# Reordering the first loads and moving the visit of the single row block in a tuned TensorE-bound kernel

## The chip, the cores and the metric

One core of one Trainium2 chip. The metric is the device time of one execution in microseconds (us), lower is better.

## The reference

Two stages on `x` of shape (8, 4224, 192). The first is a causal convolution over 7 tokens with softmaxed taps per head; the second mixes tokens with two 4224 x 4224 matrices.

```python
def _attn_ref(x, weight):                       # x (8, 4224, 192), weight (8, 7)
    w = softmax(weight)                         # (cut: written out in the reference)
    x_pad = np.concatenate([zeros(B, 6, D), x], axis=1)
    x_unf = x_pad[:, idx, :].reshape(B, S, K, H, group)
    return np.einsum('hk,bskhg->bshg', w, x_unf).reshape(B, S, D)

def _moe_ref(x, w_theta, w_tok_r, w_tok_i, w_ch):
    theta = x @ w_theta
    zr, zi = x * np.cos(theta), x * np.sin(theta)
    y = np.einsum('ts,bsd->btd', w_tok_r, zr) + np.einsum('ts,bsd->btd', w_tok_i, zi)
    u = x + y
    return u + np.maximum(u @ w_ch, 0.0)
```

## The kernel before

The source tokens are cut into 33 chunks of 128, the output tokens into 33 row blocks of 128. The row blocks are visited in units: 16 pairs and one single block (the last, block 32). A **step** is one visit of one unit. There are 58 steps; the units come round in turn, and each chunk is active for 17 consecutive steps, so that it meets every row block once. At most 11 chunks are active at a time. A step runs, for each active chunk, 14 `y` matmuls for a pair or 8 for the single block. Partial sums that have to wait for a later visit go to DRAM (`part`) and come back.

```python
    base = [0, 0, 1, 1, 2, 3, 3, 4, 4, 5, 5]
    start = [base[k % NW] + (NU + 1) * (k // NW) for k in range(NK)]   # first step of chunk k
    NSTEP = start[-1] + NU                                             # 58; NU = 17, NW = 11
    shift = (NU - 1 - (NSTEP - 1)) % NU        # the single block is visited in the last step
    ...
    def active(t):
        return [k for k in range(NK) if start[k] <= t < start[k] + NU]
    def unit(t):
        return (t + shift) % NU                # unit 16 is the single block
```

A chunk is prepared one step ahead: its `x` rows are loaded (`xw`, line 197, issued by GpSimd), convolved (`pc`, line 210, TensorE), multiplied with the angle weights (`v`, line 141) and turned into `z` (ScalarE and VectorE). Each step also loads two matrices of token weights (`st`, line 323, issued by GpSimd), which VectorE transposes (`wt`, line 336) and adds (line 348).

The residual `x` is added to a row block's sum at some time. For the units of the last round (`late`) this is done ahead of time, in DRAM, by accumulating DMAs that GpSimd issues. The step in which they are issued follows from the step number of the unit's last visit:

```python
                    far = known <= start[2 * NW - 1]
                    self.ahead.append((i, 2 * NU - NW + 2 * (t % NU) if far else start[-1],
                                       (t // NU - 1 - far) % 2))
    ...
        def add_ahead(self, i, which):
            tb = self.tbs[i]
            for cols in (slice(0, HN), slice(HN, N)):
                pool(nc.gpsimd.dma_start(                              # line 395
                    out=part[which][tb, :, cols], in_=xs[tb * P : (tb + 1) * P, cols],
                    accum_op=ALU.add,
                ))
```

While a step's matmuls are emitted, events are mixed in at given sevenths of the step:

```python
    def step_events(t):
        ...                                    # weight tasks, row loads, adds: cut
        here = [(r, i, which) for r in steps for i, when, which in r.ahead if when == t]
        for j, (r, i, which) in enumerate(here):
            found.append((1.5 + 1.8 * j, lambda r=r, i=i, which=which: r.add_ahead(i, which)))
        if t + 2 < NSTEP:
            nxt = steps[t + 2]
            for m in (1, 2):
                found.append((1.3 + 3 * (m - 1), lambda m=m: nxt.load_w(m)))
        ...                                    # outputs: cut
        if t >= NU - 2:
            new = [k for k in range(NK) if start[k] == t + 2 and k >= NW]
            for k in new:
                found.append((4.5, lambda k=k: load_chunk(k)))         # x loads
            at = 0.1
            for k in (k for k in range(NK) if start[k] == t + 1 and k >= NW):
                pos = [0, .5, 1.4, 2.2, 2.6, 3.1, 3.15, 3.4, 3.6]      # preparation of chunk k
                ...
                at += 2.3
```

Weight loads, accumulating DMAs and GpSimd's adds are chained to each other in program order (`pool(...)`); the `x` loads are not, and a scheduler places them among the others. The start-up loads `x` of chunks 0 and 1, both weights of step 0, then `x` of chunk 2, both weights of step 1; it then goes through the first 11 chunks one by one.

Of the kernel before, what the change touches and what calls it, by code (L numbers as in the profile page):

```python
# [16 lines left out]
def kernel(  # L17
# [42 lines left out]
    NU = (NT + 1) // 2  # L60
# [4 lines left out]
    assert len(base) == NW  # L65
    start = [base[k % NW] + (NU + 1) * (k // NW) for k in range(NK)]
    NSTEP = start[-1] + NU
    shift = (NU - 1 - (NSTEP - 1)) % NU

    NOSYNC = mybir.DependencyInfo(  # L70
        mybir.DependencyClass.NoSync, mybir.DependencyReason.DATA
# [203 lines left out]
    def load_chunk(k):  # L275
        if k < NK and k not in chunks:
            chunks[k] = Chunk(k, before=chunks[k - 1] if k % NW else None)
# [229 lines left out]
    steps = [Step(t) for t in range(NSTEP)]  # L507
# [72 lines left out]
    def idle(n):  # L580
        for _ in range(n):
            pe(nc.tensor.matmul(
                spare[:, 0, 0:BH], lhsT=noise[:, 0:P], rhs=noise, start=True, stop=True
            ))
# [55 lines left out]
    def more(n):  # L640

        for i in range(n):
            if need[0] is None:
                need[0] = next(flow, NK)
            if need[0] > ready[0]:
                return n - i
            need[0] = next(flow, NK)
        return 0

    steps[0].load_rows()  # L650
    for m in (1, 2):
        steps[0].load_w(m)
    load_chunk(2)
    for m in (1, 2):
        steps[1].load_w(m)
    for i in range(NW + 2):
        ch = chunks.get(i) if i < NW else None
        old = chunks[i - 1] if 0 < i <= NW else None

        def between(n):  # L660
            left = more(n)
            if 0 < i < 3:
                idle(min(left, 2))

        if ch:
            ch.conv(0)
        between(2)
        if old:
            old.theta(0)
        between(1)  # L670
        if ch:
            ch.conv(1)
        if i == 0:
            idle(4)
        ready[0] = i - 2
        between(2)
        if old:
            old.theta(1)
        if i == 1:
            for _, f in steps[0].w_tasks():  # L680
                f()
        if i + 3 < NW:
            load_chunk(i + 3)
        between(1)
        if ch:
            ch.transpose()
        if old:
            old.product(Z11)
        between(2)
        if old:  # L690
            old.product(Z21)
        between(1)
        if old:
            old.sums(0)
        between(1)
        if old:
            old.sums(1)
        between(1)
# [37 lines left out]
```

## Time and profile before

| | before |
|---|---|
| median time | 1449.51 us (1448.77 to 1449.61, 3 runs) |
| profiled span | 1446.4 us |
| TensorE busy | 1416.3 us |
| step 4 begins at | 109.17 us |
| steps 36, 40, 41: length | 26.85, 19.73, 25.67 us |
| end of step 55's y matmuls (S) | 1413.25 us |
| last y matmul ends | 1431.38 us |

A step's begin and end are found by counting the `y` matmuls (line 443) in order of time; its length here runs from the start of its first to the end of its last. The prediction below reads the rest. One more view helps: the timeline of TensorE inside step 40, the only middle step that prepares chunks while it visits the single block (start, duration, engine, line, operation, out<-in, count; in brackets the idle time before, and what ended it):

```profile
1008.71 0.83 PE L141 MATMUL v<-wth,uT 128*128 128x192 f16 x8 [0.30 <-ACT uT L151]
1011.23 0.82 PE L141 MATMUL v<-wth,uT 128*128 128x192 f16 x8 [0.48 <-ACT z L246]
```

A step on the single block has fewer `y` matmuls, so the chain that prepares a chunk (convolve, copy, transpose, copy, multiply) has less other work to hide behind, and TensorE waits for ScalarE between its links (0.30 and 0.48 us in the two rows above).

### The profile page before, as it was taken

How to read it: one execution, taken by the hardware profiler on the slowest of the kernel's cores; microseconds unless marked ns; L12 is line 12 of the kernel's file. 1: busy time of each engine (PE TensorE's matmuls, PEld its weight loads, DVE VectorE, ACT ScalarE, POOL GpSimd, SP SyncE). 2: the span in 40 equal slices, each digit the busy share in tenths (PEclk: the TensorE clock that was granted, in tenths of full speed). 3: DMA queues.
4: the chain of work that ended last, by engine and by line, in shares of the span. 5: the costliest groups of instructions: out<-in, count | busy, mean ns of one | idle time of the engine just before them, and what ended most of it. 6: DMA issues, size and time to landing. Idle time of an engine off the chain costs nothing.

```text
span 1446.4 us, 23748 instructions
## 1 busy us (share of the span) xinstructions
PE 1416.3 (98%) x9809; PEld 887.9 (61%) x9809; DVE 979.2 (68%) x1051; ACT 315.5 (22%) x379; POOL 435.1 (30%) x655
## 2 busy tenths in 40 slices
PE   7899999999999999999999999999999999999997
PEld 5556666666666666666666666666666666666665
DVE  6893555545548777866666657877777667767686
ACT  5861101111134254000000004435210110010133
POOL 7431211111233232432433342233323123213120
PEclk9999999999999999999999999999999999999999
DMA  9986756465699998998899989999999999998893
GB/s 173 227 178 145 146 103 149 90 149 97 137 231 219 214 250 217 228 254 183 213 256 213 242 143 245 228 188 234 279 216 206 209 204 221 204 203 194 166 222 125
DMA packets 272029, 281.99 MB, mean 195 GB/s; under 512 B 106672, under 2 KB 240176, under 8 KB 271920
## 3 DMA queue, kind: packets, MB, share of 16 engines
q0 software_dynamic: 162464, 92.15, 48.4%
q1 hardware_dynamic: 71824, 178.88, 35.1%
q10 hardware_dynamic: 37632, 9.44, 4.1%
q8 instruction: 77, 1.26, 0.3%
q14 instruction: 32, 0.26, 0.1%
HBM read 245.49 MB, written 108.13 MB: 244 GB/s over the span
## 4 chain that ended last, share of the span: by engine, by line
PE 89%; DVE 4%; DMA 3%; POOL 2%; ACT 1%; issue 1%; SPq 0%; DVEq 0%; ACTq 0%; POOLq 0%
PE y L443 82%; PE v L141 5%; PE pc L210 1%; PE tp L165 1%; POOL st L323 1%; DMA xw<-in_x_dram 1%; DVE z L257 1%; DVE wt L336 1%; DVE pv L408 1%; ACT z L246 1%; DVE z L251 0%; DVE pv L476 0%; DVE wt L348 0%; POOL xw L197 0%; DMA xs<-z 0%
## 5 line engine op out<-in xcount | busy, mean ns | idle before, releaser
L443 PE MATMUL y<-z,wt 128*128 128x384 f16 x7656 | 1283.6, 326 | 10.6 <-DVE pv L408 7.5
L443 PEld LDWEIGHTS <-wt 128*128 128x128 f16 x7656 | 740.8, 98 | 488.6 <-issue 10.6
L408 DVE TENSOR_TENSOR pv<-y,pv 128x768 f32<-128x768 f32 x324 | 308.9, 954 | 323.6 <-PE y L443 282.8
L336 DVE STREAM_TRANSPOSE wt<-st 128x1408 f16<-128x1408 f16 (+7 forms) x224 | 327.8, 1465 | 48.5 <-PE y L443 39.0
L323 POOL DMA_DIRECT2D st<-in_moe_w_tok_r_dram x232 | 132.5, 578 | 466.1 <-DVE wt L336 461.0
L323 POOL DMA_DIRECT2D st<-in_moe_w_tok_i_dram x232 | 132.7, 578 | 404.4 <-DVE wt L336 388.9
L348 DVE TENSOR_TENSOR wt<-wt 128x1408 f16<-128x1408 f16 (+7 forms) x216 | 176.7, 818 | 40.8 <-PE y L443 38.4
L151 ACT ACTIVATE z<-pc 128x768 f16<-128x768 f32 x65 | 53.2, 819 | 387.2 <-PE pc L210 386.9
L151 ACT ACTIVATE ub<-pv 128x768 f16<-128x768 f32 x63 | 50.2, 835 | 333.0 <-DVE pv L408 310.4
L406 ACT ACTIVATE pv<-y 128x768 f32<-128x768 f32 x66 | 54.0, 819 | 282.0 <-PE y L443 282.0
L141 PEld LDWEIGHTS <-uT 128*128 128x128 f16 x1056 | 91.0, 98 | 25.8 <-issue 7.9
L386 POOL TENSOR_TENSOR pv<-pv,xr 128x1536 f32<-128x1536 f32 x24 | 74.5, 3105 | 68.6 <-DVE pv L476 22.1
L197 POOL DMA_DIRECT2D xw<-in_x_dram x132 | 76.4, 585 | 31.0 <-DMA xw<-xw 8.7
L476 DVE SCALAR_TENSOR_TENSOR pv<-v,pv 128x768 f32<-128x768 f32 x66 | 62.9, 954 | 27.5 <-PE v L141 27.1
L257 DVE TENSOR_TENSOR z<-z 128x768 f16<-128x768 f16 x132 | 73.4, 556 | 3.6
L151 ACT ACTIVATE uT<-tp 128x1536 f16<-128x1536 f16 (+1 forms) x48 | 58.2, 1215 | 74.4 <-PE tp L165 74.4
L246 ACT ACTIVATE z<-v,half_pi 128x768 f16<-128x768 f32 x66 | 59.8, 907 | 41.2 <-PE v L141 40.8
L251 DVE TENSOR_TENSOR z<-z 128x1536 f16<-128x1536 f16 x66 | 60.0, 947 | 7.5 <-ACT z L246 7.5
L141 PE MATMUL v<-wth,uT 128*128 128x192 f16 x528 | 55.0, 248 | 4.4 <-ACT z L246 3.0
L141 PE MATMUL v<-wch,uT 128*128 128x192 f16 x528 | 54.2, 246 | 2.1 <-DVE pv L476 1.2
L246 ACT ACTIVATE z<-v 128x768 f16<-128x768 f32 x66 | 53.4, 809 | 0.0
L210 PE MATMUL pc<-xw,bands 96*64 96x192 f16 x528 | 35.8, 258 | 2.6 <-ACT bands L625 1.1
(44 smaller groups left out, 142.4 us busy)
## 6 DMA issues: line engine op xcount, KB each, us to landing
part<-pv SPq DMA_DIRECT2D x79, 768.0 KB, 4.3
pv<-part SPq DMA_DIRECT2D x79, 768.0 KB, 6.1
out_dram<-pv SPq DMA_DIRECT2D x66, 384.0 KB, 4.3
st<-in_moe_w_tok_r_dram POOLq DMA_DIRECT2D x136, 176.0 KB, 5.5
st<-in_moe_w_tok_i_dram POOLq DMA_DIRECT2D x136, 176.0 KB, 5.1
xs<-z SPq DMA_DIRECT2D x132, 96.0 KB, 4.5
xw<-in_x_dram POOLq DMA_DIRECT2D x121, 96.0 KB, 6.1
xr<-xs SPq DMA_DIRECT2D x24, 384.0 KB, 3.7
```

The lines of the kernel that those rows point to most:

```text
L141: pe(nc.tensor.matmul(v[:, k, b * D : (b + 1) * D], lhsT=tT[:, 3 * k + b + i, :], rhs=w[:, 2 * b + i, :], start=(i == 0), stop=(i == 1),))
L151: act(nc.scalar.activation(out=out, in_=in_, func=AT.Copy))
L197: nc.gpsimd.dma_start(out=self.xw[lo : lo + n, h, :, :], in_=x[:, t0 : t0 + n, :].rearrange("b s d -> s b d"),)
L246: act(nc.scalar.activation(**args))
L257: dve(nc.vector.tensor_tensor(out=z[:, o, :], in0=z[:, a, :], in1=z[:, b, :], op=ALU.subtract))
L323: pool(nc.gpsimd.dma_start(out=st[a * Q : (a + 1) * Q, 0:nb, :, 0:n] .rearrange("i r bt s -> i (r bt) s"), in_=w[self.tbs[0] * P : (self.t ...
L336: dve(nc.vector.transpose(self.w[name][:, 0 : self.n, :, :], self.st[int(name[1])][:, int(name[0]) - 1, :, 0 : self.n * Q] .rearrange("p b ...
L348: dve(nc.vector.tensor_tensor(out=self.w[name][:, 0 : self.n, :, :], in0=self.w[a][:, 0 : self.n, :, :], in1=self.w[b][:, 0 : self.n, :, : ...
L386: ins = pool(nc.gpsimd.tensor_tensor(out=self.pv[i], in0=self.pv[i], in1=self.xr[i], op=ALU.add))
L408: dve(nc.vector.tensor_tensor(out=o, in0=yv, in1=o, op=ALU.add))
L443: pe(nc.tensor.matmul(y[cn][:, q, 0:BH], lhsT=self.w[wn][:, c, :, :].rearrange("p bt i -> p (bt i)"), rhs=chunks[k].z[:, zn, q * BH : (q + ...
L476: dve(nc.vector.scalar_tensor_tensor(out=ub, in0=channel_mix(self.uT[i][:, 6 * g : 6 * g + 6, :], wch), scalar=0.0, in1=ub, op0=ALU.max, o ...
```

## The change

Its intent is twofold. In the front, `x` of chunk 2 is loaded between the two weight loads of step 0 and `x` of chunk 3 right after them, since the convolution of chunk 3 waits for its `x` (0.88 us in the profile before); five of VectorE's weight tasks of step 0 are put off until after the first product of chunk 0. In the rotation, `shift` grows by one, so that the single block is visited in the last step but one, and a pair comes last: the idea is to have less matmul work behind the last pair's long chain of output work.

```diff
-    shift = (NU - 1 - (NSTEP - 1)) % NU
+    shift = (NU - 1 - (NSTEP - 2)) % NU
...
     steps[0].load_rows()
-    for m in (1, 2):
-        steps[0].load_w(m)
+    steps[0].load_w(1)
     load_chunk(2)
+    steps[0].load_w(2)
+    load_chunk(3)
     for m in (1, 2):
         steps[1].load_w(m)
...
         if i == 1:
-            for _, f in steps[0].w_tasks():
-                f()
+            for at, f in steps[0].w_tasks():
+                if at < 2.2:
+                    f()
...
             old.product(Z11)
         between(2)
+        if i == 1:
+            for at, f in steps[0].w_tasks():
+                if at >= 2.2:
+                    f()
```

## The prediction

The forecast's sum is -0.2 (front) + 2.1 (middle) + 2.1 (end) = +4.0 us, 1453.5 us. Its 0.162 us for one `y` matmul is measured (42 in a row take 6.99 us).

> **What bounds the kernel now.** I read the busy shares and the chain first, then TensorE's waits by stretch, then timelines of the three stretches in which it waits. The page:
>
> ```profile
> PE 1416.3 (98%) x9809; PEld 887.9 (61%) x9809; DVE 979.2 (68%) x1051; ACT 315.5 (22%) x379; POOL 435.1 (30%) x655
> PE   7899999999999999999999999999999999999997
> ...
> PE 89%; DVE 4%; DMA 3%; POOL 2%; ACT 1%; issue 1%; SPq 0%; DVEq 0%; ACTq 0%; POOLq 0%
> ...
> L443 PE MATMUL y<-z,wt 128*128 128x384 f16 x7656 | 1283.6, 326 | 10.6 <-DVE pv L408 7.5
> ```
>
> TensorE is busy 98% and is 89% of the chain; only the first, second and last slices are thinner. A program of the same matmuls can therefore win or lose only where TensorE waits: 1446.4 - 1416.3 = 30 us in all. I counted y matmuls in time order (14 per active chunk in a step on a pair of row blocks, 8 in the step on the single block) to find where each of the 58 steps begins. Steps 4 to 36, from 109 to 922 us, have almost no gap. What is left is the front (0 to 109 us), step 40, and the end from about 1413 us.
>
> The front, TensorE's and VectorE's timelines:
>
> ```profile
> 26.58 0.24 PE L210 MATMUL pc<-xw,bands 96*64 96x192 f16 x1 [0.22 <-ACT z L246]
> 27.70 0.52 PE L210 MATMUL pc<-xw,bands 96*64 96x192 f16 x7 [0.88 <-DMA xw<-in_x_dram]
> 28.15 0.83 PE L141 MATMUL v<-wth,uT 128*128 128x192 f16 x8
> ```
>
> ```profile
> 15.35 0.76 DVE L336 STREAM_TRANSPOSE wt<-st 128x256 f16<-128x256 f16 x2
> 16.15 0.29 DVE L348 TENSOR_TENSOR wt<-wt 128x256 f16<-128x256 f16 x1
> ...
> 19.71 0.96 DVE L149 COPY uT<-tp 128x1536 f16<-128x1536 f16 x1 [1.58 <-PE tp L165]
> ...
> 25.59 0.96 DVE L149 COPY uT<-tp 128x1536 f16<-128x1536 f16 x1 [0.20 <-PE tp L165]
> ...
> 32.85 0.96 DVE L251 TENSOR_TENSOR z<-z 128x1536 f16<-128x1536 f16 x1 [1.57 <-ACT z L246]
> ```
>
> The convolution of chunk 3 waits 0.88 us for x: that is the wait that the first part of the change aims at. VectorE has two holes around it, 1.58 us before 19.71 and 1.57 us before 32.85, and is full between them.
>
> Two single-block steps (23, then 40) and the pair step before 40, in the table of stretches:
>
> ```profile
> 579.44:593.91 14.47, 14.47 (x92) 8.71 (x90) 12.25 (x12) 0.00 (x0) 5.14 (x5) 1.00 1.08 290
> 975.87:1002.72 26.85, 26.85 (x218) 17.30 (x215) 17.58 (x23) 12.33 (x14) 9.17 (x16) 1.00 1.10 227
> 1002.56:1022.29 19.73, 18.64 (x163) 11.77 (x162) 17.60 (x20) 12.22 (x14) 4.57 (x8) 1.00 1.00 309
> ```
>
> The columns are length, then busy us of PE, PEld, DVE, ACT, POOL. Only step 40 leaves TensorE idle (19.73 - 18.64 = 1.09 us).
>
> The end:
>
> ```profile
> 1423.43 0.95 DVE L408 TENSOR_TENSOR pv<-y,pv 128x768 f32<-128x768 f32 x1
> 1424.43 0.48 PE L443 MATMUL y<-z,wt 128*128 128x384 f16 x2 [0.36 <-DVE pv L408]
> 1429.06 2.33 PE L443 MATMUL y<-z,wt 128*128 128x384 f16 x12 [0.22 <-DVE pv L408]
> 1440.19 1.82 DVE L476 SCALAR_TENSOR_TENSOR pv<-v,pv 128x768 f32<-128x768 f32 x2 [0.91 <-PE v L141]
> ```
>
> Here y matmuls wait for VectorE to take earlier sums out of PSUM, and after the last of them a chain of casts, transposes and output sums runs to 1442.0; the last store ends the span at 1446.4.
>
> [...] the eight v matmuls of 28.15 had their operand at 26.55 (25.59 + 0.96) and yet stood behind the convolution that waited. [...] 42 in a row here take 6.99 us with 0.33 for the last, (6.99 - 0.33) / 41 = 0.162 us each. [...] a run of y matmuls waits for the reader of its tile (7.5 us in all, in the page's line). [...]
>
> **The change part by part.** The instructions are the same in number; the built program of after has TensorE's order unchanged until the middle.
>
> *Front.* GpSimd issues x of chunk 2 between the two weight loads of step 0 and x of chunk 3 right after them (from 20.96 to about 14.7 us), so x should be there at 26.58 and the 0.88 us go. But VectorE's five later weight tasks of step 0 (two transposes, three sums) move from the free time at 16.36 to behind the first product of chunk 0. They cost, start to start, 0.47 + 0.53 + 0.48 + 0.29 = about 1.7 us. Before, VectorE had 0.20 us to spare at 25.59; now the copy of chunk 2's transpose starts at 25.59 - 0.20 + 1.7 = 27.1 and ends at 28.0, and the v matmuls that need it start at 28.1, against 28.15. The wait for x turns into a wait for that copy. At 32.85 the hole of 1.57 us swallows the delay. Gain: about 0.2 us, an estimate.
>
> *The single block in the middle.* It is visited at steps 5, 22, 39, 56 in place of 6, 23, 40, 57. From the program's list of starts, the chunks then active are 11, 9, 9, 4 in place of 11, 11, 9, 2: both sum to 33, so the matmuls are equal. But new chunks are prepared during steps 22 and 39 (two each), where before only step 40 had any. What such a step loses I take from step 40: 72 y matmuls are 11.68 us; a pair step with two chunks takes 26.85, of which 126 y are 20.44, so two chunks cost 6.41; 19.73 - 11.68 - 6.41 = 1.64 us lost. Step 41 takes 25.67 where steps 7 to 15 take 25.19: 0.48 more. Together 2.1 us per event. Two events in place of one: +2.1 us.
>
> *The end.* Let S be the end of step 55's y matmuls (1413.25 before). Before, 72 y follow S (56 + 16); after, 60 (32 + 28). So S comes 12 x 0.162 = 1.95 us later. What follows S: before it was 28.75 us to the last vector instruction. After, in the built order: all is as before until VectorE's sum at S + 10.2 to 11.1 (the 1423.43 row), which frees a y tile. From there VectorE has the seven sums of step 57 with one output sum and one cast among them: 8 x 0.92 + 0.5 = 7.9 us, to S + 19.1; before, the last such sum ended at 1432.6 = S + 19.35. After the last y both programs have 30 transposes, 48 v matmuls and six output sums, two tiles alternating. Walking through them with 0.81 for ACT's copies, 0.95 for an output sum and 0.75 for eight v, I come to S + 28.9. So the 12 matmuls less after S buy nothing, since they lay beside vector work. End: 1.95 + 0.15 = +2.1 us.
>
> Sum: -0.2 + 2.1 + 2.1 = +4.0 us; 1449.5 + 4.0 = 1453.5 us.
>
> **The rivals.** (1) *The x wait really goes*: VectorE does the five tasks sooner than I walked, and 0.88 + 0.22 = 1.1 us come through. For: x was on the chain until 27.66. Against: the full VectorE to 28 us, and after it ACT and DVE without holes to 36 and 43 us. It would make 1452.6. (2) *The short step loses nothing at 22 or 39*, since step 40's loss may lie in what came with it (it prepares weights of 11 chunks for step 41: four transposes of 1.64 and four sums of 0.88 are 10.1 us of VectorE; step 39 of the changed kernel prepares 9 chunks). Then 1451.4 to 1452.5. (3) *The end is bound by TensorE*, so that the 12 matmuls count: 1451.4. (4) *A new DMA wait*: step 1's second weights are now held by the deferred transposes until about 23 us, and x of chunk 4 goes out 2.4 us later, landing near 34 by the 31.67 of before; its convolution starts at 36.72. If it slips further, 1 to 3 us are lost: 1455 to 1456.
>
> **Range and chances.** All terms are a few us, against 29 us for 2%. Rivals 1 to 3 together would bring it to about 1450; rival 4 to 1456.5. Range 1450.0 to 1456.5. Faster by over 2%: 0.005, since it is nearly the whole idle time of TensorE; within 2%: 0.985; slower: 0.01.
>
> **What would show it.** Right: no wait for x before chunk 3's convolution near 27, but its v matmuls still at 28.1 with a wait for the DVE copy; step 4 beginning within 1 us of 109.17; steps 22 and 39 each near 19.7 us long with gaps before v matmuls; the last y matmul 2 us later than 1431.4, and seven vector sums back to back before it. Wrong: step 4 beginning 2 us or more earlier (the front was bound by x after all), steps 22 and 39 without gaps, or a tail after S under 31 us (33.2 before).

## The result, and the profile after

The changed kernel took 1457.95 us in the median (1457.18, 1458.73, 1459.21 and 1453.50), the kernel before 1449.14 us in the same rounds (1448.48 to 1449.61, 4 runs). The ratio is 1.0056, 95% interval 1.0033 to 1.0078. Ratios here and below are the mean time of one kernel's runs over that of the other's of the same rounds, so not quite the ratio of the quoted medians. The class "within 2%" came true; the time lies 1.45 us above the upper end of the predicted range. The profiled run has a span of 1455.2 us, 8.8 us longer than before. All outputs are right.

The page of the changed kernel, in the order of the lines that the prediction showed (busy time by engine, shares of the chain that ended last, groups of instructions with their idle time and its main releaser), and below it one line of the view of waits by cause (total us, number of waits, longest):

```profile
PE 1418.4 (97%) x9809; PEld 887.8 (61%) x9809; DVE 976.7 (67%) x1051; ACT 315.1 (22%) x379; POOL 434.3 (30%) x655
...
PE 86%; DVE 6%; ACT 3%; DMA 3%; issue 1%; SPq 0%; POOL 0%; DVEq 0%; ACTq 0%; POOLq 0%
...
L443 PE MATMUL y<-z,wt 128*128 128x384 f16 x7656 | 1285.1, 326 | 12.2 <-DVE pv L408 9.1
L210 PE MATMUL pc<-xw,bands 96*64 96x192 f16 x528 | 35.9, 258 | 5.0 <-DMA xw<-in_x_dram 3.4
```

```profile
PE pc L210 <- DMA xw<-in_x_dram: 3.4, 1, 3.4
```

The counts are the same, but TensorE was busy 2.1 us longer for the same matmuls, and it has one new wait of 3.4 us for `x`. In the kernel before the same cause stands at 0.9 us, once, in the front. **It is now one wait, and not in the front.** There, the two stretches that the prediction described read as follows (TensorE, then VectorE):

```profile
27.84 0.83 PE L141 MATMUL v<-wth,uT 128*128 128x192 f16 x8 [0.98 <-DVE uT L149]
```

```profile
26.87 0.92 DVE L149 COPY uT<-tp 128x1536 f16<-128x1536 f16 x1
```

The convolution no longer waits for `x`; the eight `v` matmuls behind it wait 0.98 us for VectorE's copy instead. Step 4 begins at 108.88 us, 0.29 earlier.

Three steps of the changed kernel in the table of stretches: 22 and 39 (single block, two chunks prepared in each), then 36 (a pair). The columns are the stretch and its length, busy us (and instructions) of PE, PEld, DVE, ACT and POOL, the granted clock, the share of the DMA engines and GB/s:

```profile
552.47:572.20 19.73, 18.64 (x164) 11.78 (x162) 17.60 (x20) 12.21 (x14) 4.56 (x8) 1.00 1.04 321
984.95:1004.67 19.72, 18.64 (x162) 11.77 (x161) 16.18 (x20) 12.21 (x14) 7.49 (x14) 1.00 0.99 241
899.50:931.62 32.12, 28.69 (x217) 17.91 (x215) 22.51 (x28) 12.32 (x14) 9.11 (x16) 0.95 1.04 230
```

Steps 22 and 39 are what step 40 was before, as predicted. Step 36 is not: before, it took 26.85 us with no gap; now 32.12. Its TensorE timeline:

```profile
903.62 0.52 PE L210 MATMUL pc<-xw,bands 96*64 96x192 f16 x7 [3.43 <-DMA xw<-in_x_dram]
904.07 2.61 PE L443 MATMUL y<-z,wt 128*128 128x384 f16 x10
```

The wait itself is 3.43 us, and the ten `y` matmuls right after it take 2.61 us, where ten took 1.80 at this place before. The stretches of the wait and of what follows it say why (the third number from the end is the granted clock, 1.00 being full speed):

```profile
899.50:903.60 4.10, 0.69 (x5) 0.20 (x2) 2.98 (x4) 0.00 (x0) 2.27 (x4) 1.00 1.36 225
903.60:908.00 4.40, 4.38 (x27) 2.18 (x28) 0.00 (x0) 1.31 (x2) 0.00 (x0) 0.65 1.20 347
```

The granted clock was 0.65 over the 4.4 us after the wait; the trace's clock record has it at 0.50 for 3.41 us, from 904.90. So step 36 loses 32.12 - 26.85 = 5.27 us: 3.43 of wait and 1.84 of slower matmuls.

Why `x` came late is read from GpSimd's timeline, first of the kernel before, then of the changed one, at the same place (step 35, where `x` of the chunks that start at step 37 is issued):

```profile
878.08 2.29 POOL L197 DMA_DIRECT2D xw<-in_x_dram  x4
890.38 2.29 POOL L323 DMA_DIRECT2D st<-in_moe_w_tok_i_dram  x4 [10.02 <-DVE wt L336]
```

```profile
881.86 3.46 POOL L395 DMA_DIRECT2D part<-xs  x4
888.61 1.22 POOL L197 DMA_DIRECT2D xw<-in_x_dram  x2 [3.29 <-DMA st<-in_moe_w_tok_r_dram]
894.18 2.28 POOL L323 DMA_DIRECT2D st<-in_moe_w_tok_i_dram  x4 [4.34 <-DVE wt L336]
896.44 0.58 POOL L197 DMA_DIRECT2D xw<-in_x_dram  x1
898.16 0.57 POOL L197 DMA_DIRECT2D xw<-in_x_dram  x1 [1.13 <-DMA part<-xs]
```

Before, all four `x` loads of the first chunk were issued ahead of the second weight load, so its wait of 10.02 us for VectorE cost them nothing; the last of them landed at 888.49, 7.6 us before the convolution began (896.12). After, four accumulating DMAs (line 395) stand first; only two of the four `x` loads come ahead of the weight load, and the other two stand behind its wait for VectorE's transpose (4.34 us). The last is issued at 898.16, when the convolution wants `x` at about 900.2; it lands at 903.57. The accumulating DMAs also hold the loads back directly: they take 3.46 us to issue, the first `x` load then waits 3.29 us for a landing, and so even the two loads in front landed only at 899.26 and 899.47.

Where do the accumulating DMAs come from? From the rotation. Pair [0, 1], which before was visited for the last time in step 41 and had its residual added by GpSimd on an earlier visit, is now the unit of the last step, 57. That makes it `late`, and the rule `2 * NU - NW + 2 * (t % NU)` gives 34 - 11 + 2 x 6 = 35 for it. Before, the rule gave steps 27, 29 and 31, and the other case step 41. Step 35 is one in which chunks are loaded and prepared.

The end, VectorE and TensorE of the changed kernel:

```profile
1432.43 2.81 DVE L408 TENSOR_TENSOR pv<-y,pv 128x768 f32<-128x768 f32 x3
1436.49 4.73 DVE L408 TENSOR_TENSOR pv<-y,pv 128x768 f32<-128x768 f32 x5
```

```profile
1438.55 1.67 PE L443 MATMUL y<-z,wt 128*128 128x384 f16 x8 [0.25 <-DVE pv L408]
```

S, the end of step 55's `y`, is now at 1422.23 us. From 1432.43 (S + 10.2) to 1441.22 (S + 19.0) VectorE is full, and the last `y` matmuls wait for it; from S to the end of the span it is 32.97 us, against 33.15 before.

| | before | after |
|---|---|---|
| step 4 begins | 109.17 | 108.88 |
| step 24 begins | 593.74 | 597.54 (+3.80) |
| step 36 length | 26.85 | 32.12 (+5.27) |
| S | 1413.25 | 1422.23 (+8.98) |
| S to end of span | 33.15 | 32.97 (-0.18) |

### The profile page after: what moved, and what is told of

Same layout as the page of the kernel before. It is cut to its first block, busy times and chain, and to the rows that moved or that the text cites. A ratio compares the mean times of both kernels' runs of the same rounds, so it can differ in the third digit from the quotient of the medians.

```text
span 1455.2 us, 23747 instructions
## 1 busy us (share of the span) xinstructions
PE 1418.4 (97%) x9809; PEld 887.8 (61%) x9809; DVE 976.7 (67%) x1051; ACT 315.1 (22%) x379; POOL 434.3 (30%) x655
## 4 chain that ended last, share of the span: by engine, by line
PE 86%; DVE 6%; ACT 3%; DMA 3%; issue 1%; SPq 0%; POOL 0%; DVEq 0%; ACTq 0%; POOLq 0%
PE y L443 78%; PE v L141 5%; DVE pv L408 1%; ACT z L246 1%; PE pc L210 1%; PE tp L165 1%; DVE z L257 1%; DVE z L251 1%; DVE wt L336 1%; DVE wt L348 1%; DMA xw<-xw 1%; DMA xs<-z 1%; ACT uT L151 1%; ACT z L151 0%; DMA pv<-part 0%
## 5 line engine op out<-in xcount | busy, mean ns | idle before, releaser
L348 DVE TENSOR_TENSOR wt<-wt 128x1408 f16<-128x1408 f16 (+7 forms) x216 | 173.5, 803 | 43.5 <-PE y L443 41.1
L476 DVE SCALAR_TENSOR_TENSOR pv<-v,pv 128x768 f32<-128x768 f32 x66 | 62.9, 954 | 28.1 <-PE v L141 27.8
```

The source lines that it names most:

```text
L348: dve(nc.vector.tensor_tensor(out=self.w[name][:, 0 : self.n, :, :], in0=self.w[a][:, 0 : self.n, :, :], in1=self.w[b][:, 0 : self.n, :, : ...
```

## The experiments

Two theories at the start. **A: an order effect.** The residual additions that the rotation moved to step 35 push part of the `x` loads behind a weight load that waits for VectorE, and everything else of the prediction holds. **B: the rotation itself** costs more than predicted (short steps, tail), or the front part does, and the wait in step 36 is only a slip of a profile. Within A there were two more rivals: that the accumulating DMAs delay `x` in proportion to their traffic, or through waits for their landings (the changed kernel's profile shows one of 1.13 us before the last `x` load), rather than by the order.

**1. The additions of step 35 back to step 33** (changed kernel):

```diff
-  self.ahead.append((i, 2 * NU - NW + 2 * (t % NU) if far else start[-1],
+  self.ahead.append((i, min(2 * NU - NW + 2 * (t % NU), 33) if far else start[-1],
```

> The changed kernel, with the two residual adds of the last pair (four accumulating DMAs) issued in step 33 in place of step 35. Theory A (those four DMAs stand in GpSimd's queue ahead of the x loads for chunk preparation in step 36, and x comes too late): the 3.4 us wait for x in step 36 is gone, step 36 is 26.85 us long again (32.12 in the changed kernel), and the time falls to 1451.5 to 1453 us, 2.5 to 4 us over before. Rival B (the rotation as a whole loads the DMA engines more in steps 35 and 36, the adds are incidental): the wait stays at 2 us or more, time 1455 or over. Steps 22 and 39 stay 19.73 us, and from the end of step 55's y matmuls to the end of the span stays 33 us, under both.

Measured: 1452.72 us (1452.11 to 1454.02), before 1449.02, ratio 1.0030 [1.0015, 1.0045]. Step 36 is 26.85 us long again with no wait for `x`; steps 22 and 39 remain 19.73. The 5.27 us are gone, and the rotation costs what was predicted for it.

**2. The front part alone** (before, with the changed start-up):

```diff
-    shift = (NU - 1 - (NSTEP - 2)) % NU      # against the changed kernel
+    shift = (NU - 1 - (NSTEP - 1)) % NU
```

> The kernel before with the first part of the change alone (x of chunks 2 and 3 earlier, five weight tasks of step 0 later). If the wait for x only turns into a wait for the VectorE copy: step 4 begins 0.1 to 0.4 us earlier than in before (109.17), time 1448.8 to 1449.4, the same within noise. If the rival is right that the front is bound by x: step 4 begins at 108.3 or earlier, time 1448.3 or less.

Measured: 1448.23 us (1448.06 to 1449.25), ratio 1.0000 [0.9985, 1.0014]; step 4 begins at 109.04 us (109.17 before). The begin of step 4 is what the first reading expected; the median lies in the range set for the rival, but with a ratio of 1.0000 the times decide neither. A gain of a few tenths can neither be shown nor excluded. Across all profiles taken, step 4 began anywhere between 106.6 and 111.1 us, whatever the start-up. Whether the clock has a part in that was not shown: the profiles of the kernel before and of the changed one each have one stretch before step 4 in which the granted clock was 0.50, 3.41 us long (from 38.87 and from 37.91).

**3. The rotation alone** (before, with `NSTEP - 2`):

```diff
-    shift = (NU - 1 - (NSTEP - 1)) % NU
+    shift = (NU - 1 - (NSTEP - 2)) % NU
```

> The kernel before with the second part alone (the single block in the last step but one). If the two parts do not touch each other: as the changed kernel plus 0.3 us, 1454 to 1459 us, with the wait for x in step 36, steps 22 and 39 at 19.73 us. If the stall needs the changed front: no wait in step 36, about 1452.5.

Measured: 1456.20 us (1454.72 to 1460.16), ratio 1.0057 [1.0040, 1.0074], the same as the whole change. Its profile, TensorE in step 36:

```profile
905.12 0.52 PE L210 MATMUL pc<-xw,bands 96*64 96x192 f16 x7 [2.75 <-DMA xw<-in_x_dram]
```

The wait is 2.75 us here, and ten `y` matmuls after it took 1.80 us; step 36 is 29.86 us long. So the loss belongs to the rotation, and after this wait the granted clock was 1.00 (over 905.12 to 909.50).

**4. No rotation, but one pair's additions in step 35** (before; they are moved there from step 31):

```diff
-  self.ahead.append((i, 2 * NU - NW + 2 * (t % NU) if far else start[-1],
+  self.ahead.append((i, 2 * NU - NW + 2 * (t % NU) + 4 * (t == 55) if far else start[-1],
```

> The kernel before, with its two residual adds of step 31 (four accumulating DMAs) moved to step 35, nothing else. Theory A: the stall appears here too, step 36 longer than 26.85 us by 2 to 6 us, time 1451.5 to 1455. Rival B: no stall, 1449.1 as before.

Measured: 1455.08 us (1451.34 to 1456.44), before 1449.02, ratio 1.0040 [1.0021, 1.0058].

```profile
900.90 0.85 PE L210 MATMUL pc<-xw,bands 96*64 96x192 f16 x7 [4.43 <-DMA xw<-in_x_dram]
```

The kernel before, with nothing but four DMA issues moved by four steps, has the same wait at the same place, 4.43 us; step 36 is 33.81 us long, 6.96 more than before where 2 to 6 was expected, and the granted clock over the 4.1 us that followed the wait was 0.50. In GpSimd's order two of the four `x` loads stand behind the second weight load, as in the changed kernel. That is the cause without the change, and with experiment 1 the change without the cause.

**5. The additions stay in step 35, but behind the x loads** (changed kernel):

```diff
-  found.append((1.5 + 1.8 * j, lambda r=r, i=i, which=which: r.add_ahead(i, which)))
+  found.append((1.5 + 1.8 * j + 3.5 * (t == 35), lambda r=r, i=i, which=which: r.add_ahead(i, which)))
```

> The changed kernel with the four accumulating DMAs still in step 35, but 3.5 sevenths of the step later, so that the built order has them behind all eight x loads and the second weight load of that stretch. If the place in GpSimd's in-order queue is what counts (with the waits on landings that the built program puts on the loads behind them): no wait for x in step 36, time 1451.5 to 1453.5, and at most 1 us in steps 37 and 38, whose x loads now stand behind them. If it is the added traffic of 1.5 MB in that stretch: a wait for x of 2 us or more remains in steps 36 to 38, time 1455 or over.

Measured: 1453.44 us (1451.75 to 1454.09), before 1449.72, ratio 1.0029 [1.0014, 1.0044]. No wait for `x`; steps 36, 37 and 38 take 26.85, 26.91 and 26.85 us. The same DMAs in the same step are harmless when they are issued later.

**6. Half of the additions in step 35, half in 33** (changed kernel):

```diff
+  self.ahead.append((i, min(2 * NU - NW + 2 * (t % NU), 33 + 2 * i) if far else start[-1],
```

> The changed kernel with the residual adds of one of the two row blocks (two accumulating DMAs) in step 35 and the other's in step 33. In the built order of GpSimd the four x loads then stand ahead of the second weight load, as in before; with all four adds in step 35 two of the x loads had come to stand behind it. If that order is the cause: no wait for x in step 36 (0.3 us at most), time 1452 to 1453.5. If the delay grows with the traffic put ahead: about half the stall, a wait of 1 to 2.5 us, time 1453.5 to 1455.

Measured: 1452.34 us (1451.98 to 1453.50), before 1449.19, ratio 1.0019 [1.0005, 1.0032]; no wait, step 36 is 26.85 us. With two accumulating DMAs the built order has all four `x` loads ahead of the weight load. But the last of them landed at 895.32, 4.6 us before the convolution began (899.92), where the kernel before had 7.6 us to spare. A delay that grows with the DMAs in front is there too, hidden as long as time is left, so this run alone does not separate the order from the traffic.

**7. All additions in step 35 and in front, but the x loads forced ahead of the second weight load** (changed kernel; this separates the place in the order from the traffic of the accumulating DMAs and the waits for landings, which experiment 5 had moved too):

```diff
-  nc.gpsimd.dma_start(                                     # x loads
+  (pool if start[k] == 37 else (lambda ins: ins))(nc.gpsimd.dma_start(
...
-  found.append((4.5, lambda k=k: load_chunk(k)))
+  found.append((4.1 if t == 35 else 4.5, lambda k=k: load_chunk(k)))
```

> The changed kernel with the residual additions still in step 35 and still in front of the x loads, but all eight x loads of the two chunks in question forced ahead of the second weight load (built GpSimd order: four accumulating DMAs, eight x loads, four loads of the second weights); the orders of the other compute engines are unchanged. If what delays x is the place behind a weight load that waits for VectorE: no wait for x in step 36 or one of at most 0.5 us, step 36 again about 26.85 us, 1452 to 1453.5 us. If what delays x is the traffic of the accumulating DMAs or the wait for their semaphores, which stand ahead here as before: a wait of 1.5 us or more stays in step 36, and 1455 us or more.

Measured: 1452.62 us (1450.77 to 1454.70, 6 runs), before 1450.03 (11 runs), ratio 1.0021 [1.0006, 1.0036]. GpSimd's timeline, and step 36 in the table of stretches:

```profile
882.44 3.46 POOL L395 DMA_DIRECT2D part<-xs  x4
888.29 1.90 POOL L197 DMA_DIRECT2D xw<-in_x_dram  x3 [2.39 <-DMA st<-in_moe_w_tok_r_dram]
890.40 0.57 POOL L197 DMA_DIRECT2D xw<-in_x_dram  x1 [0.22 <-issue]
896.57 2.27 POOL L197 DMA_DIRECT2D xw<-in_x_dram  x4 [5.59 <-DMA xw<-xw]
899.31 2.27 POOL L323 DMA_DIRECT2D st<-in_moe_w_tok_i_dram  x4 [0.47 <-DVE z L257]
```

```profile
900.08:926.93 26.85, 26.85 (x217) 17.30 (x215) 22.60 (x28) 12.33 (x14) 8.38 (x15) 1.00 1.13 248
```

The accumulating DMAs stand at the same place and take the same 3.46 us to issue, yet the fourth `x` load goes out at 890.40, not at 898.16, and TensorE is busy for all of step 36. The orders on TensorE, VectorE and ScalarE are those of the changed kernel. So it is the place behind the waiting weight load that makes TensorE wait; with the same DMAs in front and the order put right, the loss is gone. It is gone only just: the fourth load landed at 900.36, and the convolution began at 900.50, 0.14 us later, against 7.6 us to spare before. The accumulating DMAs, and the waits for landings behind them, used up the margin; the place in the order then made the loads late.

**8. The single block visited in steps 8, 25 and 42**, so that no single block lies among the last steps or the preparing ones (before, with the additions kept at step 33 or earlier, as in experiment 1; step 7 in place of 8: additions would have read rows not yet written):

```diff
-    shift = (NU - 1 - (NSTEP - 1)) % NU
+    shift = (NU - 1 - 8) % NU
```

> The kernel before with the single block at steps 8, 25 and 42 (11 active chunks, no chunk prepared beside it, not in the last steps at all); residual adds are kept at step 33 or earlier, so none falls into step 35. From the term of the short step: steps 8, 25 and 42 lose nothing beside 14.46 us of their own, and the 2.1 us of steps 40 and 41 before are gone. From the term of the end: 84 y matmuls stand behind the end of step 55 instead of 72, that end comes 1.95 us earlier, and what follows it grows by 4 to 5 us, since VectorE has two more sums of each kind there. Together 1449 to 1450.5 us. If the end were bound by TensorE, what follows would grow by 1.95 alone and the time be 1447.

Measured: 1457.97 us (1456.98 to 1461.69), before 1449.72, ratio 1.0069 [1.0049, 1.0090]. Two parts of the expectation held in kind: single-block steps without chunks to prepare lose little (14.46, 14.46 and 15.12 us; only the third, just after the trouble below, is longer), and the tail grew: from S to the end 39.1 us, 6.0 more than before where 4 to 5 was expected, though its 12 extra matmuls are worth 1.95 us on TensorE. The total missed. The rotation moved GpSimd's additions (line 386) into step 40, which prepares chunks, and there they collided with VectorE's differences of `z` (line 257). VectorE of the kernel before, then VectorE and GpSimd of this one:

```profile
1022.93 2.34 DVE L257 TENSOR_TENSOR z<-z 128x768 f16<-128x768 f16 x4
```

```profile
1019.36 5.11 DVE L257 TENSOR_TENSOR z<-z 128x768 f16<-128x768 f16 x4
1020.64 3.41 POOL L386 TENSOR_TENSOR pv<-pv,xr 128x1536 f32<-128x1536 f32 x1 [8.70 <-DVE z L257]
```

Four of these took 5.11 us in place of 2.34 while the addition ran, and two took 3.92 in place of 1.15 at the next one: 2.77 us more each time. By these rows the excess fits a single VectorE instruction each time, 0.56 + 2.77 = 3.33 us in place of 0.56, that began 0.5 us after the addition and ended 0.4 us after it. TensorE then waited 5.6 us for VectorE in two places, 3.74 us of it in one piece, after which 16 `y` matmuls took 5.28 us, 0.33 each, where the 36 before that wait took 6.01, 0.167 each. Why VectorE took longer beside the addition was not shown. No run took the collision away, so this account rests on one profile and is not tested. The second lesson of a moved rotation: what it drags along decides its worth.

**9. to 12. Can a version beat both?** Four tries to get back what short steps lose, by spreading the preparation over more of a single-block step, where `s` is the step:

```diff
-  pos = [0, .5, 1.4, 2.2, 2.6, 3.1, 3.15, 3.4, 3.6]
+  pos = ([0, .5, 1.4, 2.2, 2.6, 3.1, 3.15, 3.4, 3.6] if s.pair
+         else [0, .7, 1.6, 2.8, 3.5, 4.0, 4.05, 4.4, 4.6])
```

On the kernel before:

> The kernel before, with the chunk preparation in a step on the single block spread over more of the step (transposes to first v matmuls 1.2 sevenths apart in place of 0.8, and so on). If step 40's loss is the latency between transposes, copy and v matmuls with too few y matmuls between (8 where a pair step has 14): step 40 falls from 19.73 to 18.3 to 18.8 us, time 1447.8 to 1448.6. If it is VectorE's load, step 40 stays 19.5 or more.

Measured: 1447.60 us (1447.30, 1447.90, 1446.41, and one run at 1456.93), before 1449.72, ratio 1.0005 [0.9972, 1.0038]. In the profile step 40 falls from 19.73 to 18.07 us and its gap is gone, but step 41 rises from 25.67 to 26.20: net 1.1 us. That VectorE's sums for step 41 now come later was the explanation; the third try tests it. The one long run keeps the times from deciding.

On the kernel before with the new front, five rounds:

> A version meant to beat both: the kernel before, with the front of the change and the spread chunk preparation in its one short step. By the sum of the two profiles (0.1 to 0.3 and 1.1 us): 1447 to 1448.3 us, against 1448.5 to 1449.5 of before; the difference is about the size of the noise.

Measured: 1449.06 us (1447.73 to 1450.32), before 1449.19 (9 runs), ratio 0.9995 [0.9983, 1.0008]. A miss for the hope of a visible gain.

The same with less spreading (`[0, .6, 1.4, 2.6, 3.1, 3.5, 3.55, 3.7, 3.9]`), which was to spare step 41:

> As the run with the front and the spread preparation, but spread less (sums at 3.7 and 3.9 sevenths in place of 4.4 and 4.6), so that VectorE is less behind at the start of step 41. If step 41's excess (26.20 in the spread run, 25.19 without any) comes from the late sums, step 41 falls to 25.7 or less with step 40 still under 18.6, and the two together to 44.0 us or less (44.27 in the spread run, 45.40 in before).

Measured: 1449.02 us (1447.02 to 1449.27), ratio 0.9991 [0.9979, 1.0004]. Step 40 takes 18.39 and step 41 27.00 us in its profile, 45.39 together as in the kernel before (45.40): another miss, for step 41 got longer, not shorter, so the late sums are not shown to be its cause.

And spread preparation on experiment 1, where two short steps are at stake:

> The changed kernel with the adds in step 33 and with the chunk preparation in single-block steps spread. It has two such steps with chunks (22 and 39) where before has one, so by the term of the short step it gains twice what the spreading gave before (1.1 us in the profile: step 40 from 19.73 to 18.07, step 41 from 25.67 to 26.20): steps 22 and 39 near 18.1 us, time 1449.5 to 1451. If the loss of those steps is elsewhere: 1452.5, unchanged.

Measured: 1456.29 us (1454.49 to 1457.49), before 1449.19, ratio 1.0047 [1.0032, 1.0063], against the expectation. Both short steps did get shorter (18.07 us each), but step 40 took 34.37 us with a new wait of 4.46 us for `x`. GpSimd in its profile:

```profile
982.83 1.15 POOL L197 DMA_DIRECT2D xw<-in_x_dram  x2
991.49 2.29 POOL L323 DMA_DIRECT2D st<-in_moe_w_tok_i_dram  x4 [7.52 <-DVE wt L336]
993.77 2.85 POOL L197 DMA_DIRECT2D xw<-in_x_dram  x5
```

In experiment 1 four `x` loads stood ahead of this weight load; here the moved events made the scheduler put two behind it. There is no accumulating DMA near. It is the same pattern, made by accident: two loads behind a weight load that waits for VectorE, here for 7.52 us.

No version tried beats the kernel before by more than the noise of these runs.

## Why the prediction was right or wrong, point by point

- **The bound: right.** TensorE has 97% busy after, and what moved is where it waits, apart from 2.1 us more of busy time, 1.84 of it in step 36, where the granted clock was 0.50 for 3.41 us.
- **The front: right in mechanism, and as far as profiles tell in size, which is below what runs resolve.** The wait for `x` turned into one for VectorE's copy. The `v` matmuls start at 27.84 (28.1 predicted), the copy at 26.87 (27.1). From chunk 0's `v` matmuls to these it takes 12.66 us before, 12.48 after and 12.49 with the front alone, a gain of 0.17 to 0.18 us (about 0.2 predicted, though its own sum leaves only 0.05). That step 4 begins 0.29 us earlier says little, as it scatters by over 4 us. The front alone gave a ratio of 1.0000. One slip changed nothing: the four times add up to 1.77 us, not about 1.7. Rival 1 fell; so did rival 4 as it was put: the convolution of chunk 4 at 36.42 has no wait.
- **The short steps and the 12 matmuls before S: right.** Steps 22 and 39 are 19.73 and 19.72 us long. Taking the front (-0.29) and step 36 (5.27) from the offset of S, 8.98 - 5.27 + 0.29 = 4.00 us is left, where 2.1 + 1.95 = 4.05 was worked out. Read directly, from the begin of step 22 to that of step 24 it takes 4.09 us more than before (the second short step and the 12 matmuls), and steps 39 to 41 together take 0.10 less. Rival 2 fell. Experiment 1, with the same two short steps and no late `x`, agrees.
- **The end: right.** VectorE's run was predicted from S + 11.1 to S + 19.1 and ended at S + 19.0; the tail is 0.18 us shorter, where 0.15 longer was said. The 12 matmuls less after S bought nothing; rival 3 fell. Experiment 8 shows the reverse case: 12 matmuls more, with the vector work that hangs on them, cost 6.0 us there, not 1.95; which part of that work costs it was not tested.
- **The step that failed** is in "The change part by part", under "The single block in the middle": it took "the matmuls are equal" and counted the loss of the short steps as all that the rotation does in the middle. It left out that the rotation also renumbers the last visits, on which the residual additions hang. They went to step 35, and a term of 5.27 us was missing: 3.43 of wait for `x` and 1.84 of lower clock. Rival 4, "a new DMA wait", named the right kind of thing, but looked for it only in the front, where a transfer had visibly moved. The prediction looked at the built program for TensorE's order; GpSimd's order at that place has the four accumulating DMAs and the split `x` loads.
- **The sum without that term was right.** -0.29 + 4.00 + 5.27 - 0.18 = 8.80 us is the difference of the two spans, but only by construction, since 4.00 is what was left over. The test is in other runs: the four variants of the changed kernel in which `x` comes in time (experiments 1, 5, 6 and 7) have medians from 1452.34 to 1453.44 us; 1453.5 was predicted.

The order as the cause of the wait is shown: by putting the additions into the kernel before (experiment 4), by taking the wait from the changed kernel in four ways, among them one that keeps the DMAs in front and changes the place alone (7). The accident of experiment 12 fits, without a control of its own. The order is not the whole: the accumulating DMAs had first used up the time to spare, and how much of that is their traffic and how much the waits for landings was not separated. The clock belongs to the same term. The three waits in step 36 read: after 2.75 us (experiment 3) ten matmuls took 1.80 us, and the granted clock was 1.00 over 4.4 us; after 3.43 us (the whole change) it was 0.65 over 4.4 us; after 4.43 us (experiment 4) 0.50 over 4.1 us. In the front it reads otherwise: the granted clock was 0.50 for 3.41 us from 38.87 in the kernel before and from 37.91 in the changed one, with no gap over 1.3 us in the 15 us ahead of it (TensorE was busy for 6.58 of the 10 us from 30 on in the kernel before). Behind a wait near 102 us, 2.46 us in the kernel before and 2.45 in the changed one, it stayed at 1.00. So the length of the last gap alone does not tell the clock in these profiles, and what does was not shown.

What stays open: why one of the four timed runs of the changed kernel took 1453.5 us and the others 1457 to 1459. The wait for `x` varied between profiles (2.75 us with the rotation alone, 3.43 with the whole change), and a wait behind which the granted clock stays at 1.00, as after the 2.75 us, would account for some of it, but timed runs carry no trace. The share of the wait for a landing (1.13 us before the last `x` load) in the 3.43 us was not measured by itself either; with the `x` loads in front of the weight load (experiment 7) waits of 2.39 and 0.22 us remained before them and no wait on TensorE.

## What to carry to other kernels

When a schedule is rotated or renumbered, list every rule that depends on the step number, not only the matmuls, and compare the built order of each DMA-issuing engine with the order before. In this kernel two `x` loads that slipped behind a weight load on GpSimd were issued only after its wait for VectorE (4.34 us), which cost 5.27 us of step 36; tie the order of urgent loads explicitly, as experiment 7 does, where a scheduler is free to choose. Look also at how long before its use a load lands: here 7.6 us of margin shrank to 4.6 and 0.14 before any time was lost. In this kernel, the 12 matmuls taken from behind VectorE's last chain shortened the tail by 0.18 us, while in front of it they are worth 1.95 us, part of the 4.00 us by which S came later beside step 36 and the front.
